# Substitution rounds of the second chunk on four quarters of the array, lone half-products on four tiles, and a later start for one step's turned keys

## The chip, the cores and the metric

The kernel runs on one core of one Trainium2 chip. TensorE (PE) multiplies, VectorE (DVE), ScalarE (ACT) and GpSimd (POOL) work elementwise, SyncE (SP) starts most of the DMAs. Each engine executes its own instructions in the order in which the program issues them; semaphores make one wait for another. The metric is the device time of one execution in microseconds. The median of three runs of the kernel before is 634.22 us (633.97 to 635.05).

## The reference

Two blocks, one after the other, all in float32. First the delta rule over 768 positions, for 4 batches and 8 heads of 48 dimensions:

```
k_n = k / (norm(k) + 1e-6)
for t in range(S):
    y[t] = q[t] @ state
    v_old = state @ k_n[t]
    state += beta[t] * outer(k_n[t], v[t] - v_old)
```

Then a feed-forward block over the 3072 tokens of 384 dimensions: `h = x @ w_in` (2048 wide), `g = max(h, 0) + alpha * min(h, 0)`, `out = g @ w_out`.

## The kernel before

**Steps.** The 768 positions are cut into twelve chunks of 64 (C). A step n is one chunk of two batches (c, bp = steps[n]), so there are 24 steps and two to a chunk. In a tile of 128 partitions, half(0) holds 64 positions of one batch of the pair and half(1) those of the other; quad(i) is a quarter of 32 partitions. The eight heads stand in the free dimension as two parities a and four pairs g, and a region of PSUM for one step has one bank for each parity (region, p[:, a, g]).

**The triangular system.** Inside a chunk, each position's value depends on the earlier ones through a triangular 64x64 matrix for each batch and head. It is inverted in blocks. grams makes the key products, VectorE weighs them (L508); eliminate inverts the diagonal blocks of four steps at a time on VectorE (L594, L600) and turns them by transpositions (L567), and placing copies the results to the tiles diag, inv and so on (L762, L765).

- From step 4 on the diagonal blocks are 32x32. The block between the two halves is then two products of 32x32 tiles for each head and batch: between_1 multiplies the off-diagonal block `right` with the transposed inverse in `diag` and ScalarE copies the result from PSUM to `mid`; between_2 multiplies that with `inv`, and ScalarE copies it to `inv` (products L791, copies L803). After that solve multiplies the right-hand side with the whole inverse (L885), VectorE weighs the result to u (L889), outputs and next_state use it (L898, L917).
- In the first and second chunk (steps 0 to 3) the inverted blocks are 16x16, and the rest is solved by three rounds of substitution. off_product makes the strictly block-triangular matrix M of a step and ScalarE copies it to `diag` (L707). A round k multiplies M with the present x (substitute, L728), and VectorE adds the right-hand side (substituted, L737): x = r + Mx, three times. M's fourth power is zero.

**Quarters of the array.** A product with 64 rows and 64 columns occupies a quarter of TensorE's array: the half of the partitions that its operands stand in gives the row half, the half that its result is written to gives the column half. The first chunk (steps 0 and 1, in first_chunk) does its rounds on all four: for parity 1 the result of one round is written to the other half of the partitions, the next round reads it there, with copies of M in `away` and of the right-hand side in `crossed`, which stand in the halves changed over. Those copies are free space of the feed-forward's tile `act`, not yet written then. The second chunk (steps 2 and 3, in second_pair) reads and writes each half in its own place, on two of the four quarters. In the products between the halves, both parities go from the same row strip to the same column strip: two of sixteen 32x32 tiles are in use for a step alone. Where one call of between holds two steps (burst_b from step 7 to 21), the two interleave on four tiles.

**Order.** The program's order is written out by hand. The feed-forward's products fill TensorE between the bursts of the attention: ffn_in (L1063), whose two or more banks are each read by ScalarE's relu (L1073) and VectorE's slope (L1075) before they are used again; ffn_out (L1106); ffn_out_fast (L1127). Its weights are converted from raw words by ScalarE (L262, L263) and VectorE (L272, L277) in the first 117 us. In second_pair, alongside weaves feed-forward products and conversions with the rounds: round 0 is followed by the Gram products of step 4, the squares of step 7 and six products; rounds 1 and 2 by those of steps 5 and 6; then the solve of both steps. Steps 4 and 5 run in attention, in four shares: at the start through_state and between_1 of the next step, then solve, grams and between_2, then outputs and next_state, then to_ffn. From step 6 (JOINED) on a step has three stretches, after burst_a, turn_round and burst_b. weave issues the pieces of several generators by their due shares of the stretch; the argument soon is the share at which the pieces in `later` start.

In the second stretch `later` holds what turn_round returns: turn_k of the step nine ahead (L479, from step 16 of the keys on), turn_q (L467) two ahead for steps before 8, the rest of weigh (VectorE's reciprocal L413 and GpSimd's L419 and L420, after ScalarE's root), and load_q for three ahead on SP's queue. For step 7 these are the keys of step 16, the queries of step 9, the weights of step 16 and the loads for step 10. The Gram products of step 16 (L502, in burst_b(7)) read those keys.

Of the kernel before, what the change touches and what calls it, by code (L numbers as in the profile page):

```python
# [28 lines left out]
ALU = mybir.AluOpType  # L29
# [3 lines left out]
C = 64  # L33
# [11 lines left out]
def kernel(  # L45
# [11 lines left out]
    nc = tc.nc  # L57

    B, H, S, D = q.shape
# [6 lines left out]
    G = H // 2  # L66
# [38 lines left out]
    def half(i):  # L105
        return slice(64 * i, 64 * i + 64)
# [193 lines left out]
    for t in range(2):  # L300
# [5 lines left out]
        out=ones, in_=ones, compare_op=ALU.is_ge, fill=1.0, base=0,  # L306
# [7 lines left out]
    for t in range(2):  # L314
# [5 lines left out]
        out=first_of, in_=ident.rearrange("p (q u e) -> p u q e", u=2, e=HB // 2)[:, 0],  # L320
# [37 lines left out]
    NE = 2  # L358
    diag = [const.tile([128, H, C], FP32, name=f"diag{i}") for i in range(NE)]
# [172 lines left out]
    LB = HB // 2  # L532
# [121 lines left out]
    def quad(i):  # L654
        return slice(HB * i, HB * i + HB)
# [43 lines left out]
    def off_product(n):  # L699

        p = ps_one()[:, 0 : H * (C - LB)].rearrange("p (b i) -> p b i", b=H)
        for b in range(H):
            for i in range(4):
                nc.tensor.matmul(
                    p[quad(i), b], turned[0][quad(i), n * H + b], mid[n % 2][quad(i), b, LB:C]
                )
        nc.scalar.copy(diag[n % NE][:, :, LB:C], p)  # L707

    def cross(n):

# [4 lines left out]
    def substitute(n, x, k, p=None):  # L715

        p = region(p, G * D, g=G)
        for g, a, t in quarters():
            frm, to, m, y = half(t), half(t), diag[n % NE][:, a * G + g], x[:, a, g]
            if n >= 2 or a == 0:  # L720
                pass
            elif k == 1:
                to = half(1 - t)
            else:
                frm, m = half(1 - t), away[n % NE][:, g]
                if k == 0:
                    y = crossed[n % NE][:, g]
            nc.tensor.matmul(p[to, a, g], m[frm], y[frm])  # L728
        return p

    def substituted(n, x, p, k):

        if k == 1 and n < 2:
            for a, y in ((0, rhs_[n][:, 0]), (1, crossed[n % NE])):
                nc.vector.tensor_tensor(out=x[:, a], in0=y, in1=p[:, a], op=ALU.add)
        else:
            nc.vector.tensor_tensor(out=x, in0=rhs_[n], in1=p, op=ALU.add)  # L737
# [40 lines left out]

    PLACING = 3

    def products(n, second, p):

        to, frm = (0, 1) if second else (1, 0)
        if second:
            x, y = mid[n % 2][:, :, 0:HB], inv[n % NE][:, :, HB:C]
        else:
            x, y = right[n % EARLY][:, 1:], diag[n % NE][:, :, 0:HB]

        def product(i, t):
            rows = quad(2 * t + frm)  # L790
            nc.tensor.matmul(p[quad(2 * t + to), i // G, i % G], x[rows, i], y[rows, i])  # L791

        return product

    def copied(n, second, p):

        to = inv[n % NE][:, :, HB:C] if second else mid[n % 2][:, :, 0:HB]
        to = to.rearrange("p (a g) i -> p a g i", a=2)

        def copies():  # L800
            for t in range(2):
                rows = quad(2 * t + (0 if second else 1))
                nc.scalar.copy(to[rows], p[rows])  # L803

        return [copies]

    def between(*wanted):

        wanted = [
            (n, second, region(p, G * HB, g=G)) for n, second, p in wanted if n < N  # L810
        ]
        todo = [products(*x) for x in wanted]
        for i in range(H):
            for product in todo:
                for t in range(2):
# [10 lines left out]
    nv, rhs_, ys, us, xts, whole = {}, {}, {}, {}, {}, set()  # L826
# [132 lines left out]
    def to_ffn(n, p=None):  # L959
# [533 lines left out]
    WY, JOINED = G * D, NJ + 2  # L1493
# [192 lines left out]
    n = 2 * W_IN_P  # L1686
# [120 lines left out]
    p = [x for x in big if x is not turned_beta][0][:, 0]  # L1807
# [8 lines left out]
    n = 12  # L1816
# [111 lines left out]
    blocks, BEGUN, SOON, LAST = eliminate(1), PIECES + 1, 11, 6  # L1928
# [9 lines left out]
    n = WHOLE + PIECES - BEGUN - SOON  # L1938
# [7 lines left out]
    blocks = eliminate(2)  # L1946
# [23 lines left out]
    n = OUT_PARTS - few - 2 * rest + 1  # L1970
# [52 lines left out]
    for n in range(JOINED, N):  # L2023
        if n == NARROW:
            banks(2, 2)
        fill, share = FILL.get(n, FILLS[n % 2]), PIECES_OF.get(n, TURNS[n % NJ])
# [86 lines left out]
```

## Time and profile before

| | |
|---|---|
| median of three runs | 634.22 us (633.97 to 635.05) |
| the profiled execution | 632.27 us |
| its span, first to last instruction | 630.5 us |
| mean granted clock of TensorE | 0.999 |
| the rounds of the second chunk | 57.2 to 69.8 us |
| lone products between halves | ten runs, 131.8 to 547.4 us |
| paired ones | fifteen runs, 200.4 to 523.0 us |

Times inside the execution count from the first instruction. A row of the timeline gives the start in us, the duration, the engine, the line of the kernel, the operation, the written and read tiles, the shape and the count of merged instructions; in brackets stands how long the engine had been idle before and what ended the wait. PEld is the loading of the stationary operand, which overlaps the products. One float32 product leaves two records on PE. Durations of merged rows run from the first start to the last end.

### The profile page before, as it was taken

Reading aid. Unit: us, or ns where it says so; the run is one execution under the profiler, and the core shown is the slowest. Engines: PE = TensorE matmul, PEld = TensorE weight load, DVE = VectorE, ACT = ScalarE, POOL = GpSimd, SP = SyncE. Lnnn points to the kernel's source line nnn. Section 1 sums busy time; section 2 is a strip of 40 time slices with the busy share of each in tenths; the row PEclk is TensorE's granted clock in tenths of the full one; section 3 lists DMA queues with packets and bytes.
Section 4 is the critical chain, followed back from the end, with each engine's and each line's share of the span. In section 5 each row is a group of like instructions: output and inputs, shape, how many; then the busy total and the mean of one; then the engine's idle time right before and its main releaser. Section 6 shows DMA issues by size and latency. Waiting matters only on the chain.

```text
span 630.5 us, 21641 instructions
## 1 busy us (share of the span) xinstructions
PE 619.3 (98%) x9116; PEld 549.2 (87%) x9116; DVE 502.6 (80%) x1219; ACT 309.5 (49%) x814; POOL 98.5 (16%) x214
## 2 busy tenths in 40 slices
PE   6999999999999999999999999999999999999997
PEld 5678887566789989989989989989999999999997
DVE  5888899969989988868978868878979579386383
ACT  6878566155544156346345446335356366353230
POOL 7021211010001000000000000000053062071350
PEclk9999999999999999999999999999999999999999
DMA  7968745112252341241342221311220300100000
GB/s 120 298 141 193 243 81 158 27 40 52 47 82 42 58 71 27 54 74 29 52 75 30 42 37 28 54 26 26 49 49 13 62 15 12 29 3 1 26 1 25
DMA packets 145968, 39.26 MB, mean 62 GB/s; under 512 B 139040, under 2 KB 142256, under 8 KB 145872
## 3 DMA queue, kind: packets, MB, share of 16 engines
q1 hardware_dynamic: 144000, 37.40, 28.9%
q8 instruction: 71, 1.16, 0.8%
q10 hardware_dynamic: 1872, 0.49, 0.4%
q14 instruction: 25, 0.20, 0.1%
HBM read 33.14 MB, written 4.72 MB: 60 GB/s over the span
## 4 chain that ended last, share of the span: by engine, by line
PE 95%; ACT 2%; DMA 1%; issue 0%; POOL 0%; DVE 0%; ACTq 0%; DVEq 0%; POOLq 0%
PE p_ffn L1063 19%; PE p_ffn L1127 10%; PE p_more L1063 8%; PE p_more L1397 8%; PE p_more L1127 8%; PE p_ffn L1106 7%; PE p_more L1313 5%; PE p_ffn L1303 3%; PE p_ffn L1397 3%; PE p_pair L860 3%; PE p_pair L791 3%; PE p_ffn L1308 3%; PE p_pair L502 2%; PE p_pair L898 2%; PE p_pair L885 2%; PE p_pair L842 2%
## 5 line engine op out<-in xcount | busy, mean ns | idle before, releaser
L1063 PE MATMUL p_ffn<-xt,w_in 128*128 128x256 f32 x528 | 122.8, 383 | 0.0
L1063 PEld LDWEIGHTS p_ffn<-xt,w_in 128*128 128x128 f32 x528 | 97.8, 190 | 13.4
L954 ACT COPY xt<-z 32x96 f32<-32x96 f32 x240 | 64.5, 269 | 49.4 <-DVE z L941 46.3
L1063 PE MATMUL p_more<-xt,w_in 128*128 128x256 f32 x240 | 55.7, 382 | 0.0
L1337 POOL TENSOR_TENSOR k_t<-k_t 128x128 f32<-128x128 f32 (+1 forms) x48 | 28.4, 592 | 166.3 <-ACT k_t L1332 163.8
L600 DVE TENSOR_TENSOR block<-block,prod 128x30 f32<-128x30 f32 (+9 forms) x150 | 50.0, 333 | 5.2
L803 ACT COPY inv<-p_pair 32x256 f32<-32x256 f32 x40 | 14.5, 363 | 74.8 <-DVE u L889 37.9
L1063 PEld LDWEIGHTS p_more<-xt,w_in 128*128 128x128 f32 x240 | 44.9, 190 | 6.3
L594 DVE TENSOR_TENSOR prod<-block 128x30 f32<-128x30 f32 (+9 forms) x150 | 48.6, 324 | 1.3
L419 POOL TENSOR_TENSOR beta_t<-beta_t,rec 128x8 f32<-128x8 f32 x24 | 7.0, 294 | 244.1 <-DVE rec L413 225.1
L1075 DVE SCALAR_TENSOR_TENSOR act<-act,al_t,p_ffn 128x256 f32<-128x256 f32 x72 | 31.1, 473 | 16.2 <-ACT act L1073 16.2
L1073 ACT ACTIVATE act<-p_ffn 128x512 f32<-128x512 f32 x36 | 21.4, 595 | 26.5 <-PE p_ffn L1063 26.2
L1337 POOL TENSOR_TENSOR block<-block 128x128 f32<-128x128 f32 (+1 forms) x48 | 28.0, 583 | 12.5 <-ACT block L1332 10.0
L1303 PE MATMUL p_ffn<-xt,w_in 128*128 128x256 f32 x96 | 29.3, 387 | 0.0
L1127 PE MATMUL p_ffn<-w_out,act 128*128 128x192 f32 x160 | 27.7, 327 | 0.0
L889 DVE TENSOR_TENSOR u<-p_pair,wgt 128x384 f32<-128x384 f32 x24 | 13.2, 553 | 17.3 <-PE p_pair L885 10.1
L1127 PEld LDWEIGHTS p_ffn<-w_out,act 128*128 128x128 f32 x160 | 26.3, 190 | 0.3
L1075 DVE SCALAR_TENSOR_TENSOR act<-act,al_t,p_more 128x256 f32<-128x256 f32 x40 | 17.3, 474 | 10.9 <-ACT act L1073 10.8
L870 DVE TENSOR_TENSOR r<-v_raw,p_pair 64x192 f32<-64x192 f32 (+1 forms) x66 | 23.2, 352 | 2.9 <-PE p_pair L860 1.8
L1127 PE MATMUL p_more<-w_out,act 128*128 128x192 f32 x128 | 22.3, 326 | 0.0
L1332 ACT COPY k_t<-p_more 128x512 f32<-128x512 f32 x16 | 9.4, 586 | 25.8 <-PE p_more L1313 18.9
L1397 PE MATMUL p_more<-w_out,act 128*128 128x192 f32 x128 | 21.5, 327 | 0.0
(275 smaller groups left out, 1478.8 us busy)
## 6 DMA issues: line engine op xcount, KB each, us to landing
w_out<-in_moe_w_in_dram SPq DMA_DIRECT2D x10, 512.0 KB, 5.5
v_raw<-in_v_dram SPq DMA_DIRECT2D x48, 96.0 KB, 2.8
kl<-in_k_dram SPq DMA_DIRECT2D x96, 48.0 KB, 2.4
out_dram<-o_sb SPq DMA_DIRECT2D x90, 48.0 KB, 1.6
space_out<-in_moe_w_out_dram SPq DMA_DIRECT2D x11, 384.0 KB, 4.2
ke_last<-in_k_dram SPq DMA_DIRECT2D x25, 96.0 KB, 3.3
qp<-in_q_dram SPq DMA_DIRECT2D x64, 32.0 KB, 2.2
w_out<-in_moe_w_out_dram SPq DMA_DIRECT2D x5, 384.0 KB, 5.8
```

The source lines that it names most:

```text
L594: nc.vector.tensor_tensor(out=prod, in0=r[:, 0:j, j : j + 1].to_broadcast([128, j, n]), in1=r[:, j : j + 1, j + 1 : HB].to_broadcast([128, ...
L600: nc.vector.tensor_tensor(out=r[:, 0:j, j + 1 : HB], in0=r[:, 0:j, j + 1 : HB], in1=prod, op=ALU.add)
L870: nc.vector.tensor_tensor(out=r[to, a], in0=v_in[to, a], in1=p[own, a, :, 0:D], op=ALU.subtract)
L954: nc.scalar.copy(to[quad(r), u, bp, t], z[quad(2 * t + u), r])
L1063: nc.tensor.matmul(p_h[:, i], w_in[:, t, (f + i) * 128 : (f + i + 1) * 128], xt[:, t], start=(t == 0), stop=(t == KT - 1),)
L1075: nc.vector.scalar_tensor_tensor(out=g[:, i], in0=g[:, i], scalar=al_t[:, f + i : f + i + 1], in1=p_h[:, i], op0=ALU.mult, op1=ALU.add,)
L1106: nc.tensor.matmul(p_o[u], gs[f // 2][:, f % 2, u * 128 : (u + 1) * 128], w_out[:, f], start=(f == 0), stop=(f == FT - 1),)
L1127: nc.tensor.matmul(p, x(i), w(i), start=(i == 0), stop=(i == FP - 1))
L1303: nc.tensor.matmul(p[:, f * 256 : f * 256 + 256], w(2, f), xt[:, 2], start=True, stop=False)
L1313: nc.tensor.matmul(q[:, j], a, b, start=True, stop=True)
L1337: nc.gpsimd.tensor_tensor(out=dst, in0=a, in1=b, op=ALU.add)
L1397: nc.tensor.matmul(p, x(i), w(i), start=(i == 0), stop=(i == FP - 1))
```

## The change

1. In off_product, two GpSimd copies fill `away` for the step, each from one half of `diag` (parity 1) to the other half.
2. In substitute, parity 1 of steps 2 and 3 is written across in rounds 0 and 2, and read in the other half, with `away`, in round 1.
3. In substituted, round 0 of these steps copies parity 1's product as it is to x with ScalarE, without the right-hand side, and VectorE adds for parity 0 alone. Round 1 is as before: x = r + M(Mr) for parity 1, back in its own place. Round 2 writes Mx across again; VectorE adds it to x for parity 1, one half at a time across the partitions, and the right-hand side for parity 0. Parity 1 so gets (1 + M)(1 + M^2)r, which is the same sum.
4. In between, where only one step is wanted (lone), parity 1's products go to the other column strip of the same half, so four tiles are in use, and ScalarE copies 32x128 four times where it copied 32x256 twice. The loop runs over g and then the parity, for paired steps too.
5. In step 7 (JOINED + 1) the second stretch's `later` starts at 0.5 of the stretch instead of 0.2.

```diff
@@ off_product
         nc.scalar.copy(diag[n % NE][:, :, LB:C], p)
+        for t in range(2):
+            nc.gpsimd.tensor_copy(
+                out=away[n % NE][half(1 - t), :, LB:C], in_=diag[n % NE][half(t), G:, LB:C]
+            )
@@ substitute
-            if n >= 2 or a == 0:
+            if a == 0:
                 pass
-            elif k == 1:
+            elif k % 2 == (1 if n < 2 else 0):
                 to = half(1 - t)
             else:
                 frm, m = half(1 - t), away[n % NE][:, g]
                 if k == 0:
-                    y = crossed[n % NE][:, g]
+                    y = crossed[n][:, g]
             nc.tensor.matmul(p[to, a, g], m[frm], y[frm])
@@ substituted
+        def add(own, a, frm, y):
+            nc.vector.tensor_tensor(out=x[own, a], in0=y[own, a], in1=p[frm, a], op=ALU.add)
+
+        whole_ = slice(0, 128)
+        if n >= 2 and k == 0:
+            nc.scalar.copy(x[:, 1], p[:, 1])
+            add(whole_, 0, whole_, rhs_[n])
+            return
+        if n >= 2 and k == 2:
+            add(whole_, 0, whole_, rhs_[n])
+            for t in range(2):
+                add(half(t), 1, half(1 - t), x)
+            return
@@ products, copied, between
-        def product(i, t):
-            rows = quad(2 * t + frm)
-            nc.tensor.matmul(p[quad(2 * t + to), i // G, i % G], x[rows, i], y[rows, i])
+        places = (to, frm if lone else to)
...
+        def product(g, a, t):
+            rows, i = quad(2 * t + frm), a * G + g
+            nc.tensor.matmul(p[quad(2 * t + places[a]), a, g], x[rows, i], y[rows, i])
...
+            own, other = (0, 1) if second else (1, 0)
             for t in range(2):
-                rows = quad(2 * t + (0 if second else 1))
-                nc.scalar.copy(to[rows], p[rows])
+                rows = quad(2 * t + own)
+                if lone:
+                    nc.scalar.copy(to[rows, 0], p[rows, 0])
+                    nc.scalar.copy(to[rows, 1], p[quad(2 * t + other), 1])
+                else:
+                    nc.scalar.copy(to[rows], p[rows])
...
-        todo = [products(*x) for x in wanted]
-        for i in range(H):
-            for product in todo:
-                for t in range(2):
-                    product(i, t)
-        return [y for x in wanted for y in copied(*x)]
+        lone = len(wanted) == 1
+        todo = [products(*x, lone) for x in wanted]
+        for g in range(G):
+            for a in range(2):
+                for product in todo:
+                    for t in range(2):
+                        product(g, a, t)
+        return [y for x in wanted for y in copied(*x, lone)]
@@ the second stretch of a step
-        stretch(fill[1], blocks, share[1], later, *extra[1], soon=0.2)
+        stretch(
+            fill[1], blocks, share[1], later, *extra[1], soon=0.5 if n == JOINED + 1 else 0.2
+        )
```

More of the change, by code (lines that the diff above doesn't have):

```diff
@@ L779, with products @@
     PLACING = 3
-    def products(n, second, p):
+    def products(n, second, p, lone):
         to, frm = (0, 1) if second else (1, 0)
+        places = (to, frm if lone else to)
         if second:
@@ L787, in products, with copied @@
             x, y = right[n % EARLY][:, 1:], diag[n % NE][:, :, 0:HB]
-        def product(i, t):
-            rows = quad(2 * t + frm)
-            nc.tensor.matmul(p[quad(2 * t + to), i // G, i % G], x[rows, i], y[rows, i])
+        def product(g, a, t):
+            rows, i = quad(2 * t + frm), a * G + g
+            nc.tensor.matmul(p[quad(2 * t + places[a]), a, g], x[rows, i], y[rows, i])
         return product
-    def copied(n, second, p):
+    def copied(n, second, p, lone):
         to = inv[n % NE][:, :, HB:C] if second else mid[n % 2][:, :, 0:HB]
```

## The prediction

> **What bounds the kernel now.** I read the page first: the busy shares and the chain of work that ended last.
>
> ```profile
> PE 619.3 (98%) x9116; PEld 549.2 (87%) x9116; DVE 502.6 (80%) x1219; ACT 309.5 (49%) x814; POOL 98.5 (16%) x214
> PE 95%; ACT 2%; DMA 1%; issue 0%; POOL 0%; DVE 0%; ACTq 0%; DVEq 0%; POOLq 0%
> ```
>
> TensorE carries 95% of the chain. Its time is what counts, so an edit that shortens its products is worth their time, as long as whoever feeds it keeps up. VectorE's 80% is a mean over unlike stages, so I then asked for the busy time of each engine by stage (columns: stretch, its length, busy time and count of PE, weight loads, DVE, ACT, POOL, the clock, DMA).
>
> ```profile
> 50.00:55.00 5.00, 5.00 (x140) 4.41 (x139) 2.79 (x8) 4.45 (x13) 0.63 (x1) 1.00 0.79 235
> 57.00:88.00 31.00, 31.00 (x604) 26.54 (x603) 28.84 (x73) 18.66 (x40) 7.11 (x16) 1.00 0.61 169
> 140.77:179.00 38.23, 38.23 (x756) 28.79 (x750) 36.77 (x95) 19.64 (x52) 2.22 (x6) 1.00 0.31 57
> ```
>
> In the second chunk's stretch (57 to 88) VectorE is busy for 28.84 of 31 us, and from 140.77 to 179 for 36.77 of 38.23. There TensorE may run ahead of VectorE only by the slack it has. So the question is not only what the products save, but how much of it VectorE lets through. I call "lead" how much earlier than before an engine is at the same instruction.
>
> **What the products save.** The same view for single lines: a round of the second chunk (L728), the solve (L885), then the products between the halves (L791).
>
> ```profile
> 57.00:59.50 2.50, 2.07 (x64) 1.94 (x64) 1.00 0.78 205
> ...
> 72.00:74.00 2.00, 1.15 (x64) 1.02 (x64) 1.00 0.78 268
> ...
> 131.00:139.65 8.65, 1.96 (x96) 1.74 (x96) 1.00 0.26 59
> 139.90:157.40 17.50, 1.39 (x64) 1.17 (x64) 1.00 0.24 48
> 157.40:177.00 19.60, 1.39 (x64) 1.17 (x64) 1.00 0.32 57
> 177.00:188.20 11.20, 1.39 (x64) 1.17 (x64) 1.00 0.54 71
> 200.00:201.30 1.30, 0.75 (x64) 0.64 (x64) 1.00 0.00 0
> 546.00:548.00 2.00, 0.69 (x32) 0.58 (x32) 1.00 0.25 59
> ```
>
> A round of two steps is 64 records (each float32 product is two) in 2.07 us on two quarters of the array. The solve has the same shape on all four quarters: 1.15. So each of the three rounds should save 2.07 - 1.15 = 0.92, together 2.76 us. The four-quarter forms exist in the trace, so this price is firm.
>
> There are ten lone runs of L791, of 32 records and about 0.69 us each: three in the row from 131, two in each of the next three, one in the last. A paired run (the row from 200) has 64 records on four tiles in 0.75, hardly more. No row shows two 32x32 tiles that share a row strip and differ in their column. Bounds: no saving at all, or, if the 0.50 that remain after the last record's 0.19 (L791's mean is 194 ns) are halved, 0.25. Paired, half the records would take (0.75 - 0.19) / 2 + 0.19 = 0.47, saving 0.22. I take 0.22, since at 64x64 the solve's tiles share strips and lose nothing. Ten runs: 2.2 us. Gross: 5.0 us.
>
> On this the Trainium skill has a rule against the change. "TensorEngine Tiling (Array Packing)", section Restrictions and Gotchas, says that different row tiles cannot access the same PSUM bank at once. In the new rounds both row halves write into one bank for each parity, so by it the rounds and the runs would save nothing and the sum would be 0. The solve writes in just that way and takes 1.15 where the rule would have it near 2.07: the trace does not bear it out.
>
> **What is added.** The rows for each:
>
> ```profile
> L1408 ACT COPY u<-p_more 128x192 f32<-128x192 f32 x4 | 1.3, 319 | 2.3 <-PE p_more L1397 2.3
> L803 ACT COPY mid<-p_pair 32x256 f32<-32x256 f32 x40 | 14.6, 364 | 5.6 <-PE p_pair L791 5.1
> L870 DVE TENSOR_TENSOR r<-v_raw,p_pair 64x192 f32<-64x192 f32 x44 | 15.5, 353 | 0.9
> L551 POOL COPY same<-right 32x256 f32<-32x256 f32 x18 | 8.9, 494 | 21.0 <-DVE right L508 20.4
> ```
>
> GpSimd: four copies of 64x192 at about 0.5 each, as soon as diag is filled, little for an engine that is busy 0.63 of 5 us from 50 to 55; round 1, the first reader, comes after 61. If they hold VectorE up, it loses at most their 2 us, and from 50 to 55 it idles 5 - 2.79 = 2.2. Cost nothing; without that cover, up to 2.
>
> ScalarE in round 0: two copies of 128x192, 0.32 each, ahead of the squares. Round 1's products now wait for them and for GpSimd's blocks; behind those on TensorE stand the Grams and the feed-forward. From the end of round 0, some 58.4, to 61.9 (below) there are 3.5 us for 0.64. ScalarE between the halves: a lone run has four copies of 32x128 instead of two of 32x256. From 319 ns at 192 columns and 364 at 256 follow 0.27 at 128, so 4 x 0.27 - 2 x 0.364 = 0.36 more. ScalarE is busy 19.64 of 38.23 there, and the products that read the copies stand a share of a step later; that hides it. Uncovered it would be 3.6 us over ten runs.
>
> VectorE: an add of 192 columns takes 0.35, by the row of 64 partitions; more partitions cost it nothing. Round 0 falls from two adds of 128x384, 1.01 in all (below), to two of 0.35: 0.3 less. Round 2 rises to three adds per step, with issue 1.1, two steps 2.2 in place of 1.02: 1.2 more.
>
> **What VectorE lets through.** The second chunk in order of time:
>
> ```profile
> 57.81 1.29 DVE L522 TENSOR_TENSOR a_t<-p_pair,minus 128x512 f32<-128x512 f32 x2
> 59.10 0.65 PE L502 MATMUL p_pair<-k_t 48*64 48x64 f32 x30
> 60.80 1.01 DVE L737 TENSOR_TENSOR v_raw<-r,p_pair 128x384 f32<-128x384 f32 x2
> 62.47 2.00 PE L728 MATMUL p_pair<-v_raw,diag 64*64 64x48 f32 x61
> 65.86 1.01 DVE L737 TENSOR_TENSOR v_raw<-r,p_pair 128x384 f32<-128x384 f32 x2
> 67.73 2.00 PE L728 MATMUL p_pair<-v_raw,diag 64*64 64x48 f32 x61
> 69.85 1.02 DVE L737 TENSOR_TENSOR v_raw<-r,p_pair 128x384 f32<-128x384 f32 x2 [0.26 <-PE p_pair L728]
> 72.57 1.15 PE L885 MATMUL p_pair<-v_raw,inv 64*64 64x48 f32 x64
> 72.97 0.87 DVE L1075 SCALAR_TENSOR_TENSOR act<-act,al_t,p_ffn 128x256 f32<-128x256 f32 x2 [0.49 <-ACT act L1073]
> 77.56 0.87 DVE L1075 SCALAR_TENSOR_TENSOR act<-act,al_t,p_ffn 128x256 f32<-128x256 f32 x2 [0.80 <-ACT act L1073]
> 82.09 0.87 DVE L1075 SCALAR_TENSOR_TENSOR act<-act,al_t,p_ffn 128x256 f32<-128x256 f32 x2 [0.25 <-ACT act L1073]
> 86.88 0.87 DVE L1075 SCALAR_TENSOR_TENSOR sums<-sums,al_t,p_ffn 128x256 f32<-128x256 f32 x2
> 88.41 0.60 ACT L1073 ACTIVATE sums<-p_ffn 128x512 f32<-128x512 f32 x1 [0.82 <-PE p_ffn L1063]
> ```
>
> Round 0: the Gram products at 59.10 reuse the bank that the first L522 frees at about 58.50, so TensorE's lead stops at 0.6, less the 0.05 that a start takes after its releaser, of the 0.92. Round 1: its input is ready by 61.5, it starts at 62.47 - 0.55 = 61.9, no wait; lead 1.47. Round 2: input at 65.86 - 0.3 + 1.01 = 66.6 for the later step, which TensorE reaches at 67.73 - 1.47 + 0.46 = 66.7; lead 2.39. Then VectorE's three adds a step begin at 69.6 - 0.3 = 69.3 (no longer waiting 0.26) and end at 71.5, against 70.87 before. The solve's second half (72.57 and half of its records, 73.07, before) waits for that: 73.07 - 71.5 = 1.5 of lead is left.
>
> VectorE now lags 0.65, but its waits of 0.49, 0.80 and 0.25 for TensorE's relus go away: by 86.88 it has a lead of about 1.0. There it ends at 87.75, and the products that reuse that bank begin just after the group whose relu runs at 88.41, about 88.15: slack 0.4. So TensorE's lead stops at about 1.35. That is the worth of the rounds, of 2.76 gross; I allow 0.6 to 2.0.
>
> After it come three lone runs (131 to 139.65), 0.66: a lead of 2.0.
>
> ```profile
> 140.77 0.35 DVE L870 TENSOR_TENSOR r<-v_raw,p_pair 128x192 f32<-128x192 f32 x1 [1.82 <-PE p_pair L860]
> 156.70 0.69 DVE L522 TENSOR_TENSOR a_t<-p_pair,minus 128x512 f32<-128x512 f32 x1
> ...
> 157.44 0.69 PE L502 MATMUL p_pair<-k_t 48*64 48x64 f32 x32
> 175.67 0.83 DVE L1075 SCALAR_TENSOR_TENSOR act<-act,al_t,p_ffn 128x256 f32<-128x256 f32 x2
> 176.97 0.60 ACT L1073 ACTIVATE act<-p_ffn 128x512 f32<-128x512 f32 x1 [1.19 <-PE p_ffn L1063]
> 179.55 0.56 DVE L889 TENSOR_TENSOR u<-p_pair,wgt 128x384 f32<-128x384 f32 x1 [0.56 <-PE p_pair L791]
> 195.15 0.76 DVE L479 STREAM_TRANSPOSE k_t<-ke_pair 128x256 f32<-128x256 f32 x2
> 195.57 0.60 ACT L1073 ACTIVATE act<-p_ffn 128x512 f32<-128x512 f32 x1 [1.49 <-PE p_ffn L1063]
> 196.96 0.83 DVE L1075 SCALAR_TENSOR_TENSOR act<-act,al_t,p_ffn 128x256 f32<-128x256 f32 x2
> 199.36 0.69 PE L502 MATMUL p_pair<-k_t 48*64 48x64 f32 x32
> ```
>
> At 140.77 VectorE still waits for TensorE, so it inherits the 2.0. From there to 179 it has no wait, and at 157.39 it ends the mask that the products at 157.44 need: slack 0.05. Both lone runs before that point give nothing. Of the two behind it one gets through: the bank read until 176.50 is reused at 176.8, 0.25 of slack. The run at 178.8 adds 0.22 (VectorE had 0.56 to spare at 179.55), those at 187.4 and 546.7 the same. Sum: 1.35 + 0.66 + 0.22 + 0.66 = 2.9 us.
>
> The later start in step 7 puts the transposes of keys and queries behind the last L1075, which began at 196.96 though its relu was done at 196.17. That frees up to 0.8 us where VectorE is late; it saves no time by itself, and keeps the lead. With them move the root of the norms, VectorE's reciprocal, GpSimd's two products and SP's loads of the queries of two steps on, all read in a later part of the step or after it. The risk is the products at 199.36, which need L479, done at 195.9 before.
>
> The profiled execution took 632.27, the median shown is 634.22: 632.27 - 2.9 = 629.4 there, and 634.22 - 2.9 = 631.3 in the median, which I predict.
>
> **Rivals.** (a) Row halves that write one bank take turns: no saving, the additions hidden, 634.2. For it speaks no row; against it the 1.15. (b) 32x32 tiles in one strip do not overlap: rounds alone, 1.35, so 632.9. The missing row is all that speaks for it. (c) VectorE gives way, because its work shifts too: the gross 5.0, 629.2; against it the 0.05 at 157.44. (d) L479 comes to stand behind all that VectorE has to do up to 199.4 and takes its 0.76: TensorE waits 0.8 there, plus the 0.2 by which it is ahead of VectorE: 2.9 - 1.0 = 1.9, so 632.3. Against it: half of the stretch's work still comes after the new place. (e) Slower: the new order g before parity makes neighbouring products of L791 change bank or column each time, and products of 32 columns are too short to hide what those of 48 hide. With 20 ns more a record the fifteen paired runs (steps 7 to 21) lose 15 x 16 x 0.02 = 4.8 (16 records a strip), the lone ones gain nothing, the rounds keep 1.35: 637.7. It outweighs the rounds from 6 ns a record on. Against it: the solve changes both at no cost.
>
> **How the numbers follow.** Chances: forecast 0.55, a 0.08, b 0.10, c 0.10, d 0.07, e 0.10. The forecast's own range is 629.8 to 632.6, from 0.6 to 2.0 for the rounds and 0 to 0.25 a run. The whole range goes from c's end to a's: 629.0 to 634.4, leaving out e. A measurement of this kernel tells about 0.2%, 1.3 us, from no change. Faster: forecast, c, d and half of b, less 0.04 of the forecast's low end, 0.73; same: a, the other half of b, that end, 0.17; slower: e, 0.10.
>
> **What would show it.** A round at 1.15 for 64 records; a lone run near 0.47, the paired ones still 0.75; round 2's adds ending after the solve could have started; a wait of TensorE for L522 near 155; nothing waiting for GpSimd; L1075 ahead of L479 in step 7. The prediction is wrong if lone runs stay at 0.69, paired ones grow, or TensorE waits behind L479.

## The result and the profile after

The changed kernel takes 631.14 us (median of 21 executions, 629.45 to 634.90) where the kernel before takes 633.31 (21 executions, 632.05 to 635.06). The ratio is 0.9967, with a 95% interval of 0.9956 to 0.9977: 2.1 us less (1.5 to 2.8).

The page of the profile after, its busy shares and its chain of waits:

```profile
PE 617.4 (98%) x9116; PEld 545.5 (86%) x9116; DVE 504.0 (80%) x1223; ACT 312.4 (50%) x836; POOL 99.9 (16%) x218
PE 87%; DVE 5%; ACT 3%; DMA 2%; issue 1%; SPq 1%; ACTq 0%; DVEq 0%
```

TensorE is busy for 1.9 us less, and its part of the chain falls from 95% to 87%; the largest share of that goes to VectorE, from 0% to 5%. That is the first thing to see: TensorE has come so far ahead that it now runs into VectorE in places. The stages, as busy time in windows (columns as in the prediction): first the rounds (now L732), then the solve (L910), then the products between the halves (L809).

```profile
59.50:62.00 2.50, 1.28 (x64) 1.15 (x64) 1.00 0.68 189
64.00:67.00 3.00, 1.15 (x64) 1.02 (x64) 1.00 0.78 178
69.00:71.50 2.50, 1.15 (x64) 1.02 (x64) 1.00 0.95 261
...
73.00:75.60 2.60, 1.98 (x64) 1.51 (x64) 1.00 0.95 339
...
131.00:141.00 10.00, 1.36 (x96) 1.03 (x96) 1.00 0.27 61
...
200.00:202.00 2.00, 0.75 (x64) 0.64 (x64) 1.00 0.04 8
546.00:548.00 2.00, 0.45 (x32) 0.34 (x32) 1.00 0.32 81
```

The second and the third round take 1.15 instead of 2.07 and the first 1.28, a lone run takes 0.45 (1.36 / 3) instead of 0.69, and a paired one 0.75 as before. But the solve, whose products were not touched, went from 1.15 to 1.98. The timeline of the stretch shows why:

```profile
61.99 0.31 ACT L742 COPY v_raw<-p_pair 128x192 f32<-128x192 f32 x1
63.59 0.35 DVE L738 TENSOR_TENSOR v_raw<-r,p_pair 128x192 f32<-128x192 f32 x1
63.97 0.32 ACT L742 COPY v_raw<-p_pair 128x192 f32<-128x192 f32 x1 [1.67 <-DVE v_raw L738]
64.32 0.35 DVE L738 TENSOR_TENSOR v_raw<-r,p_pair 128x192 f32<-128x192 f32 x1 [0.39 <-ACT v_raw L742]
...
68.72 1.01 DVE L754 TENSOR_TENSOR v_raw<-r,p_pair 128x384 f32<-128x384 f32 x2
69.32 1.15 PE L732 MATMUL p_pair<-v_raw,diag 64*64 64x48 f32 x64 [0.15 <-DVE v_raw L754]
...
72.37 0.34 DVE L738 TENSOR_TENSOR v_raw<-r,p_pair 128x192 f32<-128x192 f32 x1
73.24 2.12 PE L910 MATMUL p_pair<-v_raw,inv 64*64 64x48 f32 x64
73.90 0.74 DVE L738 TENSOR_TENSOR v_raw<-v_raw,p_pair 64x192 f32<-64x192 f32 x2
74.69 0.54 PEld L910 LDWEIGHTS p_pair<-v_raw,inv 64*64 64x64 f32 x26 [0.19 <-DVE v_raw L738]
```

In round 0 copy and add take turns: the second copy waits for the first add (1.67 idle on ScalarE), and the second add for the second copy (0.39 idle on VectorE). In round 2 the last of VectorE's six adds ends at 74.64 (73.90 + 0.74), and the last 26 weight loads of the solve start right behind it, at 74.69. The table of TensorE's waits does not show this in full, since products in flight cover the gaps; the rows of the weight loads do.

**How leads are counted from here on.** For one and the same instruction I take its start in the profile before and in another profile, both counted from the feed-forward products ahead of the rounds:

```profile
54.85 2.43 PE L1063 MATMUL p_ffn<-xt,w_in 128*128 128x256 f32 x10
...
131.84 0.69 PE L791 MATMUL p_pair<-diag,right 32*32 32x32 f32 x32
178.24 0.63 PE L885 MATMUL p_pair<-r,inv 64*64 64x48 f32 x32
548.40 0.70 PE L1303 MATMUL p_ffn<-xt,w_in 128*128 128x256 f32 x2
```

These rows are of before; the same instructions in the profile after:

```profile
57.65 2.43 PE L1088 MATMUL p_ffn<-xt,w_in 128*128 128x256 f32 x10
...
133.62 0.45 PE L809 MATMUL p_pair<-diag,right 32*32 32x32 f32 x32
179.25 0.63 PE L910 MATMUL p_pair<-r,inv 64*64 64x48 f32 x32
548.42 0.70 PE L1328 MATMUL p_ffn<-xt,w_in 128*128 128x256 f32 x2
```

The profiled execution after comes 2.80 us late to the first of them and 0.02 late to the last: the lead there is 2.78 us. So two spans that are almost equal (630.5 and 630.7) hide 2.78 us of gain behind a start that was worse in this execution. The leads of all kernels, in us, at the solve of the second chunk (72.57 in the time of before), behind it (73.97), and at later products:

| kernel | late at 54.85 | 72.57 | 73.97 | 131.84 | 139.70 | 178.24 | 188.03 | 199.36 | 548.40 | ratio to before (95%) |
|---|---|---|---|---|---|---|---|---|---|---|
| after | 2.80 | 2.13 | 1.16 | 1.02 | 1.75 | 1.80 | 2.56 | 2.55 | 2.79 | 0.9967 (0.9956 to 0.9977) |
| before_again | 1.45 | 0.00 | 0.00 | 0.00 | 0.00 | 0.00 | 0.00 | 0.01 | 0.01 | one execution |
| rounds_only | 1.23 | 2.12 | 1.15 | 1.07 | 1.07 | 1.08 | 1.37 | 1.12 | 1.12 | 0.9971 (0.9956 to 0.9986) |
| lone_only | 0.20 | 0.00 | 0.00 | 0.00 | 0.72 | 0.81 | 1.58 | 1.09 | 1.33 | 0.9969 (0.9953 to 0.9984) |
| early_keys | 1.41 | 2.10 | 1.20 | 0.96 | 1.68 | 1.77 | 2.53 | 2.01 | 2.25 | 0.9967 (0.9951 to 0.9982) |
| parity_outer | 3.83 | 2.13 | 1.16 | 0.92 | 1.20 | 1.29 | 1.09 | 1.09 | 1.09 | 0.9983 (0.9968 to 0.9998) |
| copies_first | 1.28 | 2.35 | 1.65 | 1.55 | 2.27 | 2.35 | 3.12 | 3.12 | 3.36 | 0.9953 (0.9938 to 0.9968) |
| last_in_place | 1.81 | 1.22 | 1.22 | 1.22 | 1.94 | 2.02 | 2.78 | 2.78 | 3.02 | 0.9986 (0.9968 to 1.0003) |
| later_words | 1.23 | 1.96 | 1.96 | 1.25 | 1.97 | 2.06 | 2.82 | 2.81 | 3.05 | 0.9976 (0.9951 to 1.0001) |
| rounds_relieved | 2.62 | 1.84 | 1.84 | 1.17 | 1.89 | 1.98 | 2.75 | 2.74 | 2.81 | 0.9972 (0.9959 to 0.9985) |
| words_in_gaps | 0.13 | 1.73 | 1.73 | 1.72 | 2.45 | 2.50 | 3.27 | 3.27 | 3.51 | 0.9954 (0.9937 to 0.9971) |
| copies_and_last | 1.43 | 0.82 | 0.82 | 0.82 | 1.54 | 1.60 | 2.37 | 2.36 | 2.60 | 0.9962 (0.9948 to 0.9975) |
| sums_early | 1.75 | 1.21 | 1.21 | 1.12 | 1.84 | 2.88 | 3.65 | 3.63 | 3.86 | 0.9934 (0.9917 to 0.9951) |

The intervals are 0.7 to 1.6 us to either side, so differences below that are read from the leads, not from the ratios. A lead leaves out the first 55 us and comes from one execution, so it need not equal the ratio. Executions whose mean granted clock is 0.997 or less are longer in the median (24 of 88 of before in the experiments, 635.03 against 633.58 for the others), and of last_in_place, whose ratio falls short of its lead of 3.02, 7 of 12 are of that kind.

### The profile page after: what moved, and what is told of

The parts are those of the page before. It is cut to its first block, busy times and chain, and to the rows that moved or that the text cites. A ratio compares the mean times of both kernels' runs of the same rounds, so it can differ in the third digit from the quotient of the medians.

```text
span 630.7 us, 21675 instructions
## 1 busy us (share of the span) xinstructions
PE 617.4 (98%) x9116; PEld 545.5 (86%) x9116; DVE 504.0 (80%) x1223; ACT 312.4 (50%) x836; POOL 99.9 (16%) x218
## 3 DMA queue, kind: packets, MB, share of 16 engines
q8 instruction: 71, 1.16, 0.7%
## 4 chain that ended last, share of the span: by engine, by line
PE 87%; DVE 5%; ACT 3%; DMA 2%; issue 1%; SPq 1%; ACTq 0%; DVEq 0%
PE p_ffn L1088 16%; PE p_ffn L1152 10%; PE p_more L1088 8%; PE p_more L1422 8%; PE p_more L1152 8%; PE p_ffn L1131 5%; PE p_more L1338 5%; PE p_ffn L1328 3%; PE p_ffn L1422 3%; PE p_ffn L1333 3%; PE p_pair L885 2%; PE p_pair L923 2%; PE p_pair L809 2%; PE p_pair L910 2%; PE p_pair L502 2%; PE p_pair L867 2%
## 5 line engine op out<-in xcount | busy, mean ns | idle before, releaser
L1088 PE MATMUL p_ffn<-xt,w_in 128*128 128x256 f32 x528 | 123.2, 384 | 0.1
L1088 PEld LDWEIGHTS p_ffn<-xt,w_in 128*128 128x128 f32 x528 | 97.6, 190 | 14.1 <-issue 0.4
L1088 PE MATMUL p_more<-xt,w_in 128*128 128x256 f32 x240 | 55.7, 382 | 0.0
L1088 PEld LDWEIGHTS p_more<-xt,w_in 128*128 128x128 f32 x240 | 44.9, 190 | 6.3
L1100 DVE SCALAR_TENSOR_TENSOR act<-act,al_t,p_ffn 128x256 f32<-128x256 f32 x72 | 31.0, 471 | 14.5 <-ACT act L1098 14.4
L826 ACT COPY inv<-p_pair 32x256 f32<-32x256 f32 x30 | 10.9, 363 | 59.2 <-DVE u L914 35.5
L1152 PE MATMUL p_ffn<-w_out,act 128*128 128x192 f32 x160 | 27.7, 327 | 0.0
L1152 PEld LDWEIGHTS p_ffn<-w_out,act 128*128 128x128 f32 x160 | 26.2, 190 | 0.3
L1100 DVE SCALAR_TENSOR_TENSOR act<-act,al_t,p_more 128x256 f32<-128x256 f32 x40 | 17.3, 474 | 10.9 <-ACT act L1098 10.7
L1152 PE MATMUL p_more<-w_out,act 128*128 128x192 f32 x128 | 22.3, 326 | 0.0
```

Of the source, the lines that this page charges most:

```text
L1088: nc.tensor.matmul(p_h[:, i], w_in[:, t, (f + i) * 128 : (f + i + 1) * 128], xt[:, t], start=(t == 0), stop=(t == KT - 1),)
L1100: nc.vector.scalar_tensor_tensor(out=g[:, i], in0=g[:, i], scalar=al_t[:, f + i : f + i + 1], in1=p_h[:, i], op0=ALU.mult, op1=ALU.add,)
L1152: nc.tensor.matmul(p, x(i), w(i), start=(i == 0), stop=(i == FP - 1))
```

## The experiments

**The start: before once more.** No edit.

> The kernel before once more, for its start. In the profile of before TensorE reached 56 us up to 3.8 us earlier than in those of the changed kernels, though nothing ahead of 46 us was changed. Theory: the start differs from run to run (loads, and stalls of TensorE at 34 to 40 us that no wait explains): this profile comes 0.5 to 3 us later to the same point than the first one. Rival: the change lengthens the start: this profile is within 0.3 us of the first one.

It comes 1.45 us late to 54.85 and then stays within 0.01 us of the first profile to the end. So the first 55 us differ from execution to execution, and behind them two executions of one kernel agree to a hundredth. Each changed kernel has one profile only, so whether the pauses within its rounds, below, are the kernel's or the execution's is not shown. The waits of TensorE in the first twelve and from 34 to 42 us, in the profiles of before, of after and of this run in turn:

```profile
PE p_pair L332 <- DMA ke_pair<-in_k_dram: 0.5, 1, 0.5
...
PE p_pair L885 <- issue: 0.5, 1, 0.5
```

```profile
PE p_pair L332 <- DMA space_out<-in_beta_dram: 1.0, 1, 1.0
...
PE p_pair L732 <- issue: 1.8, 1, 1.8
```

```profile
PE p_pair L332 <- DMA space_out<-in_beta_dram: 1.4, 1, 1.4
...
PE p_pair L885 <- issue: 0.8, 1, 0.8
```

A load that lands sooner or later, and a pause of 0.5 to 1.8 us in which TensorE waits for nothing that the profile shows. That the changed kernels start later on average is not excluded by these profiles, but it cannot be told from this spread: before alone ranges over 3 us.

**The parts alone.** Each of the two kernels leaves the other change, and the due share of step 7, as before.

```diff
@@ rounds_only: between
-        lone = len(wanted) == 1
-        for g in range(G):
-            for a in range(2):
+        for i in range(H):
@@ lone_only: substitute
-            if a == 0:
+            if n >= 2 or a == 0:
...
-            elif k % 2 == (1 if n < 2 else 0):
+            elif k == 1:
```

> Only the substitution rounds of the second chunk are changed; the products between the halves and the due share of step 7 are as before. Theory: the rounds are worth what VectorE's three adds a step leave of them, about 1.1 us, and that lead is kept to the end: ratio to before about 0.998, and in the trace TensorE's lead is near 1.1 after the solve and at 130 us and at the end. Rival: what the rounds gain is given back at the mask near 157 us, where the slack was 0.05; then the time is as before (ratio 1.000) and only the lone runs paid.

> Only the products between the halves are changed (four tiles for a lone step, pairs before parities); rounds and due share as before. Theory: ten runs fall from 0.69 to 0.45 us, but the three that lie between 144 and 159 us give nothing since VectorE sets the pace there: 3 x 0.24 before 140 us, 0 to 0.25 at 168 us, 4 x 0.24 after 178 us, together 1.4 to 1.9 us, ratio about 0.9975. Rival: all ten pay, 2.4 us, ratio 0.996. Second rival: none of those before 178 us pays, 1.0 us, ratio 0.9985.

The rounds alone lead by 2.12 us ahead of the solve, 1.15 behind it, and keep 1.12 to the end; the rival, that this is given back near 157 us, falls. (The 0.28 that come before 188 and the 0.25 that go by 199 are taken up below.) The lone runs alone bring 0.72 before 140 us, 0.09 from there to 178 (four runs that take 0.45 instead of 0.69), and 1.33 at the end, a little below the expected 1.4 to 1.9, since 0.49 is lost between 188 and 199. The next kernel shows at what. Of the 1.33, 0.28 do not come from the lone runs (see the lone runs below).

**The due share of step 7.**

```diff
-            fill[1], blocks, share[1], later, *extra[1], soon=0.5 if n == JOINED + 1 else 0.2
+            fill[1], blocks, share[1], later, *extra[1], soon=0.2
```

> The changed kernel, but with the second stretch of step 7 started at 0.2 as before. Theory: the later start saves no time by itself: within 0.3 us of the changed kernel, 631.1. Rival: with TensorE ahead, the transposes of the keys ahead of the last slope operation keep a PSUM bank from TensorE: it waits up to 0.8 us near 197 us, and the time is up to 0.8 longer, 631.9.

The lead falls from 2.53 to 2.01 between 188 and 199 us, where the changed kernel keeps its own (2.56 to 2.55). The timeline of this kernel:

```profile
194.56 0.76 DVE L479 STREAM_TRANSPOSE k_t<-ke_pair 128x256 f32<-128x256 f32 x2
...
196.38 0.83 DVE L1100 SCALAR_TENSOR_TENSOR act<-act,al_t,p_ffn 128x256 f32<-128x256 f32 x2
196.88 1.96 PE L1152 MATMUL p_ffn<-w_out,act 128*128 128x192 f32 x10 [0.17 <-DVE act L1100]
```

and of the changed kernel:

```profile
195.62 4.07 PE L1152 MATMUL p_ffn<-w_out,act 128*128 128x192 f32 x24
...
196.47 0.86 DVE L1100 SCALAR_TENSOR_TENSOR act<-act,al_t,p_ffn 128x256 f32<-128x256 f32 x2
198.37 0.78 DVE L479 STREAM_TRANSPOSE k_t<-ke_pair 128x256 f32<-128x256 f32 x2
199.62 0.69 PE L502 MATMUL p_pair<-k_t 48*64 48x64 f32 x32
```

The later of the feed-forward products L1152 read what the slope operation L1100 writes. With the transposes ahead of it TensorE has to wait in the middle of these 24 records; with them behind it L1100 is in time, and the transposes are still done at 199.15, ahead of their reader at 199.62. So my theory for this run (no time by itself) was wrong and the rival nearly right: by the leads the later start is worth 0.5 us once TensorE has a lead. The ratios (0.9967 for both) do not tell the two kernels apart. That it brings nothing to a kernel without a lead is argued, not run.

**The order of the lone products.** The loop over parities is put outside that over pairs again.

```diff
-        for g in range(G):
-            for a in range(2):
+        for a in range(2):
+            for g in range(G):
```

> The changed kernel, but the products between the halves run over the parity first and the pair second, as before the change, so that eight heads' products in a row go to one column strip. Theory: two tiles of a strip overlap only where neighbouring products go to different columns: a lone run is back at 0.6 to 0.69 us, and about 1.5 us of the gain are lost, 632.6. Rival: the queue of TensorE looks past neighbours, or the four tiles alone matter: 0.45 as in the changed kernel and 631.1. Paired runs at 0.75 in both.

Its products L809 before 140 us (three lone runs), in a window as above:

```profile
130.00:143.00 13.00, 1.80 (x96) 1.47 (x96) 1.00 0.20 47
```

A lone run takes 1.80 / 3 = 0.60, between 0.69 on two tiles and 0.45 with neighbours on different columns: the overlap comes mostly from neighbouring products, as expected. The starts of the single records say more: in the first ten and the last ten of the 32 two records start every 0.03 us or slower, as on two tiles in before, and the 0.09 are saved in the twelve between, where the run passes from one parity, and so from one column strip, to the other. Three runs before 140 us bring 0.28 here and 0.73 in the changed kernel. Of the 1.70 that this kernel lacks at the end, 0.66 lie outside the lone runs: the 32 records of L867 at 189 us (L842 of before) took 1.29 instead of 0.63, with a pause of 0.36 in which TensorE waits for nothing that the profile shows.

**The wait between copy and add.** Both of ScalarE's copies are issued before both adds.

```diff
-            add(whole_, 0, whole_, rhs_[n])
-            return
+            return lambda: add(whole_, 0, whole_, rhs_[n])
...
+            for add in adds:
+                if add:
+                    add()
```

> The changed kernel, but in round 0 ScalarE's copies of both steps are issued ahead of VectorE's adds of both. In the changed kernel copy and add take turns (copy of step 2, add of step 2, copy of step 3, add of step 3) and VectorE idles 0.39 us ahead of the second add. Theory: this wait is why round 0 brought VectorE nothing; without it VectorE ends its adds of round 2 about 0.4 us earlier, and TensorE loses 0.7 in the solve instead of 1.06: time 0.3 to 0.4 us less than the changed kernel. Rival: VectorE waits just as long for another thing, or the lead is lost again by 90 us: no difference.

Its timeline in round 0 and the solve:

```profile
60.47 0.53 ACT L742 COPY v_raw<-p_pair 128x192 f32<-128x192 f32 x2
62.08 0.61 DVE L738 TENSOR_TENSOR v_raw<-r,p_pair 128x192 f32<-128x192 f32 x2
...
71.51 1.85 PE L909 MATMUL p_pair<-v_raw,inv 64*64 64x48 f32 x64
```

The two adds run as one block of 0.61, with no wait (1.08 from 63.59 to 64.67 in the changed kernel). The solve loses 0.70 instead of 0.97, the rounds are worth 1.55 instead of 1.02, and the lead at the end is 3.36 instead of 2.79. The theory holds, and by the lead a little more than expected: the short wait ahead of round 2 went too (2.35 ahead of the solve instead of 2.13). Why a copy for one step has to wait for the add of the other, whose x is another tile, the rows do not say; both read parts of one PSUM tile.

**The third round's crossing.** Round 2 writes parity 1 in its own place, with two adds a step.

```diff
+            elif n >= 2 and k == 2:
+                pass
...
-            for t in range(2):
-                add(half(t), 1, half(1 - t), x)
+            add(whole_, 1, whole_, x)
```

> The changed kernel, but round 2 of steps 2 and 3 writes parity 1 in its own place (two quarters) and VectorE needs two adds a step, not three. Theory: TensorE pays 0.92 for the round and gets back what the solve lost by waiting for the adds (1.06): the same time as the changed kernel within 0.3 us, so the third round's crossing was worth nothing. Rival: the solve's wait has another cause and stays: 0.9 us slower than the changed kernel.

```profile
71.38 0.34 DVE L740 TENSOR_TENSOR v_raw<-r,p_pair 128x192 f32<-128x192 f32 x1
...
72.17 0.34 DVE L740 TENSOR_TENSOR v_raw<-v_raw,p_pair 128x192 f32<-128x192 f32 x1
...
73.16 1.15 PE L911 MATMUL p_pair<-v_raw,inv 64*64 64x48 f32 x64
```

The four adds are done within 1.13 us (71.38 to 72.51), before the solve, and the solve is back at 1.15. TensorE pays 0.92 for the round and gets it back: 1.22 against 1.02. So in the changed kernel the third crossing was worth nothing: it bought 0.92 us of TensorE with adds that cost TensorE 0.97. This rests on the leads; the medians (0.9986) would make this kernel the worse one, with intervals that overlap.

**Taking work off VectorE.** The three conversion parts between rounds 1 and 2 are made after the second chunk; then the same with copies first; then the latter without the conversion that opens the next stretch.

```diff
-                alongside(6, 3)
+                alongside(6, 0)
...
-    convert_on = chain(conv_in, part(conv_out, 10))
+    convert_on = chain(conv_in, part(conv_out, 7))
...
-        (behind_relus(ffn_in(1), part(conv_out, PARTS_OUT - 10 - LAST)), IN_PARTS - 4),
+        (behind_relus(ffn_in(1), part(conv_out, PARTS_OUT - 7 - LAST)), IN_PARTS - 4),
...
words_in_gaps, in behind_relus:
-        next(converted, None)
```

> The changed kernel, but the three conversion parts between rounds 1 and 2 (1.3 us of VectorE between its adds of round 1 and of round 2) are made after the second chunk, beside the feed-forward products. Theory: VectorE's lateness alone makes TensorE wait in the solve, so that wait goes (1.06 to 0.1 at most), the lead after the solve is near 2.1 instead of 1.1 us, and the time is about 1 us less than the changed kernel. Rival: the next reuse of a bank (88 us, slack 0.15 in the changed kernel) or the conversions' new place takes it back: within 0.3 of the changed kernel.

> Both of the foregoing: copies ahead of the adds in round 0, and the three conversion parts later. Theory: the wait of 0.15 ahead of round 2 goes too; the rounds pay nearly their gross 2.76, some 1.4 us less than the changed kernel. Rival: as for later conversions, what is won is lost at the next reuse of a bank.

> As the kernel with copies first and later conversions together, but the stretch after the second chunk does not begin with a conversion: its first comes after three feed-forward products. In the two kernels with later conversions ScalarE made one conversion more at 85.3 us, ahead of the relu at 86.4; VectorE idled 0.86 for that relu and TensorE 0.47 for VectorE, which cost 0.6 of the lead. Theory: with that conversion out of the way the lead of 1.8 to 2.3 after the solve stays, and the kernel is 0.3 to 0.8 us faster than the one with copies first (profile lead at 130 us 1.9 to 2.4 in place of 1.54). Rival: the next conversion or slope operation takes it: lead at 130 us near 1.2 to 1.5 again.

In the first two the wait in the solve is gone: the lead is the same ahead of it and behind it (1.96 and 1.84). But 0.7 us are lost by 131.84, so for the time the rivals were right. The timeline of later_words, from three engines:

```profile
85.34 0.58 ACT L262 ACTIVATE w_out<-w_out 128x384 uint32<-128x384 uint32 x1
85.96 0.56 ACT L263 ACTIVATE w_out<-w_out 128x384 f32<-128x384 f32 x1
86.42 0.57 ACT L1098 ACTIVATE sums<-p_ffn 128x512 f32<-128x512 f32 x1
...
87.03 0.87 DVE L1100 SCALAR_TENSOR_TENSOR sums<-sums,al_t,p_ffn 128x256 f32<-128x256 f32 x2 [0.86 <-ACT sums L1098]
...
88.05 2.83 PE L1088 MATMUL p_ffn<-xt,w_in 128*128 128x256 f32 x12 [0.47 <-ACT w_out L263]
```

A conversion that left the queues near 70 us stands in ScalarE's queue at 85 us, ahead of the relu; the relu is late, so VectorE is, and so the bank comes free late. (The row names L263 as the releaser of the products, but VectorE's L1100 ends at 87.90, 0.15 ahead of them, and reads the bank: the name of a releaser is inferred.) Without that conversion the lead stays, 1.73 and 1.72. It is below the expected 1.9 to 2.4, because TensorE paused for 0.25 in round 0 and for 0.19 behind round 2 with nothing to wait for; against copies_first it is a draw (0.9954 and 0.9953), so the 0.3 to 0.8 us expected over it are not shown.

**Both remedies of the adds.** Copies first and round 2 in its own place.

> The changed kernel with copies first in round 0 and round 2 in its own place. Theory: VectorE is never late, so TensorE gets the whole of two rounds, 2 x 0.92 = 1.84, less what the reuse of the bank at 88 us takes: lead at 130 us 1.4 to 1.8, equal to or up to 0.3 better than copies first alone (1.54). Rival: VectorE's adds still come last: 1.2 as with round 2 in place alone.

Inconclusive: the lead is 0.82. TensorE paused for 0.7 us within round 0 (PE p_pair L734 from "issue" in the table of its waits), after which the lead is -0.10; the rest brings 0.92, one whole round.

**VectorE between 141 and 179 us.** On the base of copies_first, three sums of the weights are issued one stretch earlier.

```diff
-        (part(blocks, 6), 6),
+        (part(blocks, 6), 6), (weight_sums(0, 0, 3), 3),
...
-        extra = [(weight_sums(0, 0, 3), 3)] if n == NJ else []
+        extra = []
```

> The kernel with copies first, and three of VectorE's sums of the weights (0.95 us each, in step 4 between 144 and 154 us so far) are issued in the stretch before, between 131 and 140 us, where VectorE idles 2.7 and 1.0 us. Theory: VectorE sets the pace from 141 to 179 us, and this alone is why the lone runs at 144, 153, 158 and 168 us gave next to nothing (TensorE's lead 2.26 at 139.7 and 2.35 at 178.5 with copies first). With 2.85 us less there the four runs pay, 0.9 us: lead at 178.5 about 3.1, and the time 0.7 to 0.9 less than with copies first. Rival: the wait moves to another releaser in the stretch (the mask or the right-hand side at 140 us, now behind the sums): lead at 178.5 at most 2.5, the same time.

First the solve at 157 us in the changed kernel, then in this one:

```profile
157.48 0.96 PE L910 MATMUL p_pair<-r,inv 64*64 64x48 f32 x32
158.50 0.69 PE L502 MATMUL p_pair<-k_t 48*64 48x64 f32 x32
```

```profile
156.33 0.68 PE L909 MATMUL p_pair<-r,inv 64*64 64x48 f32 x32
156.83 0.66 PE L502 MATMUL p_pair<-k_t 48*64 48x64 f32 x32
```

The solve and the Gram products behind it follow each other in 0.50 us instead of 1.02. From 139.70 to 178.24 the lead grows by 1.04 (1.84 to 2.88), where it grew by 0.05 in the changed kernel: four runs of 0.24, paid in full. The theory holds. This kernel has the largest lead of all and the lowest ratio, 0.9934 of before (4.2 us less), though the interval overlaps those of copies_first and words_in_gaps, and though a pause of 0.7 us at the Gram products behind round 2 ("issue" again) took the gain of that round. It was not run together with words_in_gaps.

## Why the prediction was right, and which terms were off

**The rounds: 1.35 predicted, 1.02 measured.** The price of 0.92 held for two rounds (1.15 each). The first took 1.28, which cost nothing, since the first stop held: the lead was 0.55 at the Gram products behind round 0, as the mask's bank allowed, and 0.52 at round 1. The step that failed is "Round 0 falls from two adds of 128x384 to two of 0.35: 0.3 less". The durations were right, but the two adds did not run one after the other: copy and add waited for each other in turn, and VectorE reached round 1's adds 0.06 late (68.72 - 65.86 - 2.80) instead of 0.3 early. What follows up to the solve is off by this: TensorE waited 0.15 ahead of round 2, had 2.13 ahead of the solve instead of 2.39, and 1.16 behind it instead of 1.5. The next term, the stop of 1.35 at the bank of 88 us, was then hardly reached: the lead fell from 1.16 to 1.02. copies_first removes just that wait and gets 1.55, so 1.35 is no fixed stop: it moves with VectorE, whose lead at 86.88 was 0.84 in the changed kernel and 1.37 there. The prediction took "about 1.0"; its own figures give 0.9 (0.49 + 0.80 + 0.25 - 0.65).

**What I had costed at nothing.** The GpSimd copies were done by 54.4 us, and their first reader starts at 64.75: nothing. ScalarE's copies I had hidden by "3.5 us for 0.64"; as work they fit, but the second ended at 64.29, only 0.46 before the products that read both. Their price came by the order in which they were issued, not by their length.

**The lone runs.** 0.24 each instead of 0.22. The three before 140 us gave 0.73 (0.66 predicted); from there to 157.44 nothing, as predicted (1.75 to 1.74); one of the two behind it should have come through with 0.22, and 0.06 did. Those two brought the lead to 2.18 at 167.7, but from 174.2 to 177.0 it fell back to 1.80: in the changed kernel the weight loads of L1088 stopped for 0.42 and for 0.23 us and went on only behind VectorE's L1100 (its end at 174.87, the next load at 174.99; its end at 177.55, the next load at 177.67). In sums_early, where VectorE has less to do, nothing is lost there. The last three gave 0.72 (0.66). Between 178 and 188 us 0.28 more appeared that I had not foreseen: the 32 records of L842 at 186.6 took 0.92 in both profiles of before and 0.63 in the changed one. In before the thirteenth of them starts 0.19 after the twelfth, where none of the others in the row is more than 0.06 behind the one ahead of it; in parity_outer the twelfth starts 0.58 after the eleventh, and in the other changed kernels, rounds_only and lone_only too, there is no such stop. So neither the rounds nor the lone runs brought these 0.28; what makes the stop stays open.

**The later start of step 7.** "It saves no time by itself, and keeps the lead" was right, and the measured price of doing without it is 0.5 us, within the 0.8 named. Rival (d), that TensorE would wait for L479, falls: it is done 0.47 ahead of its reader.

**The other rivals.** (a) falls: row halves that write one bank overlap, and the rounds and lone runs both pay. By the rule of the Trainium skill's "TensorEngine Tiling (Array Packing)", Restrictions and Gotchas, the new rounds would have stayed at 2.07; the trace has 1.15. The Trainium skill's "PSUM — Partial Sum Buffer", section "PSUM bank collisions raise a hardware error", quotes the same rule and gives as measured a narrower one: writes from different row tiles collide in the same bank and the same 32 partitions, which the crossed products do not share; with that the trace agrees. (b) falls: 0.45. (c), the gross 5.0, was out of reach for the reason given, VectorE; sums_early shows that with copies first and less work on VectorE 3.86 come through. (e) falls: paired runs stay at 0.75 to the end.

In sum 2.9 was predicted and 2.78 measured in the trace; the medians say 2.1 (1.5 to 2.8). The forecast was near mostly because it asked at each stage what the next buffer or operand was waiting for, and let only that much through. But part of the agreement is luck. The rounds came out 0.33 short and the two runs before 178 us 0.16, and the 0.28 of L842 made up for more than half of that: without them the trace would say 2.5. The time itself, 631.3 forecast and 631.14 measured, agrees better than the gain does, since the 634.22 it starts from was the median of three, and that of 21 executions is 633.31. And the range of 629.8 to 632.6 does not follow from its bounds, 0.6 to 2.0 for the rounds and 0 to 0.25 a run: 0.6 and no run would give 633.6.

## What to carry to other kernels

When the bound engine is sped up, price what it gains from the slack of its next operand and its next buffer, stage by stage; here half of the gross gain of 5.0 us was lost where another engine works almost without a break. Where two engines write parts of one tile or read parts of one region, try issuing all of the one's instructions before the other's: here taking turns cost a wait of 1.67 us on ScalarE and of 0.39 on VectorE. And where a lead is to be kept, look at what stands ahead of the operation that frees the next buffer, on every engine of that chain: the same conversion cost 0.7 us ahead of a relu (later_words) and nothing where it came three products later (words_in_gaps).

## What the hardware showed that I had not expected

How far two 32x32 tiles in one row strip overlap goes by the order of the products: a lone run takes 0.45 where neighbours alternate between the column strips, 0.60 where they change once in the middle, and 0.69 on one column strip. And TensorE pauses at times with nothing to wait for in the profile: for up to 2.0 us at a time at 34 to 41 us in every profile (for 0.2 in words_in_gaps, 0.5 in the first one of before), and in several of the changed kernels for 0.2 to 0.7 in or behind one round of the second chunk. After the one of 1.8 us the granted clock fell. Windows of the profile after:

```profile
34.00:36.00 2.00, 0.65 (x23) 0.43 (x22) 0.60 (x3) 1.74 (x5) 1.90 (x3) 1.00 0.54 101
36.00:38.00 2.00, 1.59 (x63) 1.58 (x66) 1.01 (x3) 1.95 (x5) 0.58 (x3) 0.72 0.67 127
38.00:40.00 2.00, 2.00 (x59) 1.91 (x52) 1.50 (x4) 0.36 (x1) 0.00 (x0) 0.50 0.51 91
```

TensorE pauses from 34.6 to 36.4, and the clock column (third from the right) then reads 0.72 and 0.50, where before shows 1.00 throughout. In the profile of parity_outer a pause of 2.02 us ends at 36.1, and the clock reads 0.50 from 38 to 44. In the other profiles no such pause is longer than 1.30, and the clock there reads 1.00. So a long pause seems to cost twice: from 33.9 to 38.0 us in the time of before the profile after loses 2.26 us against it, though before pauses for 0.48 there itself. After its own pause of 1.77 that leaves 0.97 (2.26 + 0.48 - 1.77), an estimate of what the lower clock cost. Such pauses make single profiles differ by as much as the change under study brings.
